# Another written order of the opening words in a fused delta-rule and hard-swish kernel

## The chip, the cores and the metric

The kernel runs on one core of a Trainium2 chip. The metric is the device time of one execution in microseconds, read as the median of three runs. A core has five engines with a queue of instructions each: TensorE (PE; its weight loads are shown apart as PEld), VectorE (DVE), ScalarE (ACT), GpSimd (POOL) and SyncE (SP), which here issues nearly all transfers between HBM and SBUF. Each queue runs strictly in the order in which the instructions were written, and an instruction whose input is not there yet holds up everything behind it in its queue.

## What is computed

Two stages. The first is a delta rule: for each of 4 batches and 8 heads a 48 x 48 state is carried through 768 tokens.

```python
k_n = k / (np.linalg.norm(k, axis=-1, keepdims=True) + 1e-06)
for t in range(S):
    y[:, :, t] = np.einsum('bhd,bhde->bhe', q[:, :, t], state)
    v_old = np.einsum('bhde,bhd->bhe', state, kt)
    state = state + bt[:, :, :, None] * np.einsum('bhd,bhe->bhde', kt, vt - v_old)
```

The second takes the result as 3072 tokens of 384 numbers through a feed-forward block of width 2048 with a hard swish between its two products.

```python
h = x @ w_in                      # 384 -> 2048
relu6 = np.clip(h + 3.0, 0.0, 6.0)
g = h * relu6 / 6.0
return (g @ w_out).astype(np.float32)   # 2048 -> 384
```

q, k, v and beta come as float32; the two weight matrices come as float64.

## The kernel before

**Tiles.** The 768 tokens are cut into 24 tiles of 32 tokens; one tile of all four batches fills the 128 partitions. Within a tile the recurrence becomes products of small matrices: the scores of the keys (`sc`, L533), a strictly lower triangular matrix per head (`L`, L544), its inverse (`X`), the state's contribution (`ks`, L792), the new values (`pz`, L813), the output (`py`, L813) and the state update (`su`, L924). Tiles form groups: tile 0 alone, then tiles 1 to 4, 5 to 8 and so on. The inverse of a group is made on VectorE, 128 problems side by side, by a substitution of pairs of ops (L716/L721 for the first full group, which works on 16 x 16 halves; L745/L750 for later groups) between two large transposes (L455, L459). The halves of tiles 1 to 4 are then joined by two groups of small matmuls per tile (`join`, L670). Tile 0 has an inverse of its own, by products on TensorE (`product`, L582).

**Feed-forward.** Two tiles make a block of 256 tokens. `up` multiplies by `w_in` in 16 units per block (L980; the first block in two halves of 16 units each, words `ua` and `ub`), with one ScalarE op (L987) and one VectorE op (L990) behind each unit. `down` multiplies by `w_out` (L1140, later L1204). The PSUM tiles of `up`, `down` and of most small products share a ring of four slots, so a unit can't start before the L990 of an earlier one has read its slot.

**Weights.** Each matrix comes in 8 pieces of 768 KB (`load_w`, L323), 16 in all, as float64 words. They become float32 by bit operations: ScalarE scales the high word (L348), makes a rounding carry from it (L351) and from the low word (L353); VectorE shifts and masks the high word (L368); GpSimd adds the carry (L375). The words `a` (three to a piece) and `c` (two to a piece: L368, then L375) step through these two generators.

**What sets the order.** The opening, up to about 175 us, is written out as a string of words, `ORDER` (L23 to L41). Each word advances a named generator by one step, and so decides where the step's instructions stand in every queue at once; a count behind a star repeats it. Behind the string follow loops for tiles 5 to 23, which are planned by costs in the code. The words: `k`, `q`, `v`, `B`, `w` issue one load each (keys, queries, values, beta, a weight piece); `n` are the norms of the keys (L393 to L417), `p` the preparation of a tile (L496, L510, L518, L533, L544), `m` the mask product (L472), `b` the scaled keys (L484), `x` the inverse of tile 0 or the join of a tile, `h` the chain of a tile, `y` its output, `i1` and `i2` the substitutions of the groups 1 and 2, `ua`, `ub`, `u` the units of the feed-forward, `ra`, `rb`, `ru` the ScalarE op behind a unit, `ga`, `gb`, `gu` the VectorE op behind it, `e` an eviction, `z` and `s` settings.

The word's meaning in code:

```python
def do(word):
    if word in gens:
        next(gens[word])
    elif word[0] == "r":
        relus[word[1]].pop(0)()
    elif word[0] == "g":
        pending[word[1]].pop(0)()
...
with tc.manual_schedule():
    for word in ORDER.split():
        word, _, n = word.partition("*")
        for _ in range(int(n or 1)):
            do(word)
```

The waits between engines are put in by the framework from what each instruction reads and writes. Loads take turns on eight completion semaphores, in the order of the words.

Of the kernel before, what the change touches and what calls it, by code (L numbers as in the profile page):

```python
# [20 lines left out]


ORDER = """  # L23
k*2 B*3 k*2 n0 k*2 z B s*2 n0*6 k*2 q*2 n1 q n1 q w k p0 z*3 k n1*2 k*2 n1*2 z p0*2 s k p0*3 a k a
m0 a n2 m1 p0 x0*2 w q x0 n1 x0*3 c n2 k s p1*2 a s*2 k q s*2 x0 n2 k*2 c x0 n2 x0 w q a*3 q p1 n2
k*2 a x0 m2 p1 c p1 n2*3 b1 q b0 s p1 x0 q w x0 n2 q*2 c*2 x0 n4 k p1 k p2*2 x0*2 a c a*2 q*3 a w v
p3*2 q x0 q n4 p2*2 c p2 v n4*2 a*3 z v n4 c m3 v c p2 n4*2 q p2 k b2 h0 c h0 w a*2 h0 p4*2 a m4 p3
q*4 h0 q k w p4*2 c*2 v*2 p3 k p3*3 k*2 p4*2 v*2 p4 m6 k a w a c w i1*3 k i1*7 a i1*4 v i1*2 k b3 k
y0 c y0*3 ua*2 ra*2 i1*3 w v ga v a*3 i1*2 ua i1 h1 i1 q w ua ra ua i1 ra*2 ga i1 k ua a ra ga i1 ga
ua ra ua ra i1 ga i1*4 ua ga n5 x1*2 k x1 c a ra v a ga x2 k*2 ga*2 ua*2 x1 ra*2 x1*2 ua h1*2 n5 k  # L30
ga ra ga*2 h1 c y1*2 ua ra w ga ua ra x2 n5 ga y1*2 ua ra ga h1 v*3 n5*2 k y1*2 ua ra x2 ub*2 n5
rb*2 h1 x3 ga c a*2 w a h2 y2 v gb ub rb gb x2 gb ub*2 n5*2 b4 rb n5 x2*2 h2 gb rb gb m5 n5*2 ub rb
gb v c q*2 v q*5 n5 ub n5 rb gb h2 y2 c h2 q ub y2*2 rb ub p5 b5 h2 rb gb*2 a*2 x3 p5 ub y2*2 k p5*2
h2 rb h3 p5 gb h3 ub*2 q rb gb rb gb ub a x3 p6 v x4 x3 rb gb ub p7 rb gb y3 c*2 v p7*2 y3 v p7*2 b6
x3 q x3 ub h3 p6*2 c p5*2 rb gb k m7 w p6 h3 u p6 k*2 q*3 a*2 y3 a p6 c y3 v y3*2 u n9 v k q a c u*2
ru gu w k a c a*2 x4 c ru p7 a c gu k u a p7 p6 m8 u*3 a k u*2 k h3 w ru*2 a*2 gu*2 x4 c x4 k c p8 k
a*2 u ru k h3 u*2 h4 ru a b8 gu k gu y4 p8*3 u h4 k*2 c q k*9 q u p8*2 k ru k*2 gu k c n9 q u q*2 p8
k*2 b7 n9*2 x4 i2 u x4 q i2*2 q ub ru gu u rb gb i2*2 h4*2 u*2 i2 ru i2*6 y4 i2 gu i2*7 u i2 ru gu
i2 u*3 ru i2*4 gu ru i2*2 v i2 gu u*4 ru c i2 u*2 i2 gu i2*3 q i2*5 y4 n9 i2 e*2 n9*2 i2*4 q i2 y4 e
n9 u ru i2*3 u h4 i2 ru*2 gu h4 u n9 i2*2 u i2 e i2*6 y4 u k n9*3 u gu i2 y4 n9 i2 p9 q i2*2 gu  # L40
"""  # L41


# [1478 lines left out]
```

## Time and profile before

| | |
|---|---|
| median of three runs | 671.5 us (671.26 to 672.24) |
| the profiled execution | 669.61 us |
| its span, first to last instruction | 667.8 us |
| PE busy | 635.8 us (95%) |
| DVE busy | 462.8 us (69%) |
| ACT busy | 260.5 us (39%) |
| POOL busy | 227.5 us (34%) |
| mean granted TensorE clock | 0.986 |

By stretches, busy time of each engine, the clock granted to TensorE and the share of the DMA engines:

| us | PE | DVE | ACT | POOL | clock | DMA |
|---|---|---|---|---|---|---|
| 0 to 10 | 1.80 | 5.01 | 3.73 | 6.56 | 1.00 | 0.57 |
| 10 to 20 | 6.10 | 5.78 | 7.39 | 5.72 | 1.00 | 1.08 |
| 20 to 30 | 7.32 | 5.70 | 7.99 | 7.16 | 1.00 | 0.86 |
| 30 to 40 | 4.24 | 5.72 | 5.81 | 7.49 | 0.73 | 0.97 |
| 40 to 50 | 7.29 | 6.04 | 7.00 | 4.90 | 0.76 | 0.78 |
| 50 to 60 | 7.65 | 9.21 | 5.59 | 0.94 | 0.75 | 0.99 |
| 60 to 70 | 9.97 | 7.48 | 6.47 | 3.96 | 0.90 | 0.51 |
| 70 to 80 | 9.35 | 5.54 | 6.92 | 1.84 | 1.00 | 0.16 |
| 110 to 120 | 10.00 | 4.81 | 6.95 | 6.97 | 1.00 | 0.43 |

How to read it: a wait is shown with what ended it. "issue" names a wait for nothing that the profile shows. A row of the order of time has the start, the duration, the engine, the line of the program, the operation, the tiles it writes and reads, and in brackets the idle time just before it with its releaser. A float32 matmul of the program is recorded as two matmuls and two weight loads.

### The profile page before, as it was taken

How to read it: one execution, taken by the hardware profiler on the slowest of the kernel's cores; microseconds unless marked ns; L12 is line 12 of the kernel's file. 1: busy time of each engine (PE TensorE's matmuls, PEld its weight loads, DVE VectorE, ACT ScalarE, POOL GpSimd, SP SyncE). 2: the span in 40 equal slices, each digit the busy share in tenths (PEclk: the TensorE clock that was granted, in tenths of full speed). 3: DMA queues.
4: the chain of work that ended last, by engine and by line, in shares of the span. 5: the costliest groups of instructions: out<-in, count | busy, mean ns of one | idle time of the engine just before them, and what ended most of it. 6: DMA issues, size and time to landing. Idle time of an engine off the chain costs nothing.

```text
span 667.8 us, 26310 instructions
## 1 busy us (share of the span) xinstructions
PE 635.8 (95%) x11544; PEld 568.2 (85%) x11544; DVE 462.8 (69%) x1110; ACT 260.5 (39%) x516; POOL 227.5 (34%) x336
## 2 busy tenths in 40 slices
PE   2768999999999999999999999999999999999997
PEld 2657887776689988988999989999999999999997
DVE  5658653689545687747888857988748998456353
ACT  4765677322142232232244244245244144153250
POOL 5762144202511130363165255055052241331330
PEclk9967999999999999999999999999999999999999
DMA  7887355302040030031030030020020020000000
GB/s 175 201 213 208 77 112 137 69 13 46 17 91 14 3 73 3 2 76 34 3 70 7 2 67 9 2 62 2 3 49 2 2 50 2 19 21 3 26 1 25
DMA packets 88499, 33.27 MB, mean 50 GB/s; under 512 B 80160, under 2 KB 83232, under 8 KB 88384
## 3 DMA queue, kind: packets, MB, share of 16 engines
q1 hardware_dynamic: 88128, 31.29, 20.9%
q8 instruction: 91, 1.49, 0.9%
q10 hardware_dynamic: 256, 0.30, 0.2%
q14 instruction: 24, 0.20, 0.1%
HBM read 26.84 MB, written 4.72 MB: 47 GB/s over the span
## 4 chain that ended last, share of the span: by engine, by line
PE 92%; DVE 2%; SPq 2%; DMA 2%; issue 1%; ACT 1%; DVEq 0%; ACTq 0%
PE po L1204 28%; PE ph L1052 21%; PE ph L980 16%; PE po L1140 6%; PE ks L792 3%; PE pt L510 3%; PE pz L813 3%; PE su L924 3%; PE py L813 3%; PE sc L533 3%; PE yt L859 1%; SPq L168 1%; DMA spare<-in_moe_w_in_dram 1%; PE pi L670 1%; DMA w_out<-in_moe_w_in_dram 1%
## 5 line engine op out<-in xcount | busy, mean ns | idle before, releaser
L1052 PE MATMUL ph<-xT,w_in 128*128 128x128 f32 (+1 forms) x560 | 121.3, 321 | 0.7 <-issue 0.7
L980 PE MATMUL ph<-xT,w_in 128*128 128x256 f32 (+1 forms) x576 | 118.7, 357 | 3.2 <-DVE g L990 2.2
L1204 PE MATMUL po<-w_out,g 128*128 128x192 f32 x640 | 110.6, 326 | 0.0
L980 PEld LDWEIGHTS ph<-xT,w_in 128*128 128x128 f32 x576 | 96.9, 197 | 15.9 <-DVE g L990 2.6
L1204 PEld LDWEIGHTS po<-w_out,g 128*128 128x128 f32 x640 | 104.6, 190 | 0.5
L1052 PEld LDWEIGHTS ph<-xT,w_in 128*128 128x128 f32 x560 | 91.1, 191 | 6.0 <-issue 0.8
L1016 POOL TENSOR_TENSOR g<-g 128x256 f32<-128x256 f32 x112 | 67.9, 608 | 82.9 <-ACT g L1066 78.5
L1204 PE MATMUL po<-spare,g 128*128 128x192 f32 x480 | 86.7, 332 | 0.0
L1204 PEld LDWEIGHTS po<-spare,g 128*128 128x128 f32 x480 | 77.2, 190 | 1.8
L987 ACT ACTIVATE g<-ph,halves 128x256 f32<-128x256 f32 (+1 forms) x96 | 41.8, 437 | 84.6 <-PE ph L980 84.5
L1214 POOL TENSOR_TENSOR o<-o,u 128x192 f32<-128x192 f32 x18 | 13.2, 732 | 175.7 <-ACT o L1211 97.2
L1066 ACT ACTIVATE g<-ph 128x512 f32<-128x512 f32 x56 | 33.5, 597 | 82.2 <-PE ph L1052 82.2
L990 DVE SCALAR_TENSOR_TENSOR g<-g,ph 128x256 f32<-128x256 f32 (+1 forms) x96 | 35.1, 371 | 40.3 <-ACT g L987 40.1
L1190 DVE TENSOR_TENSOR g<-g 128x512 f32<-128x512 f32 x80 | 55.6, 716 | 5.6 <-PE po L1204 5.6
L745 DVE TENSOR_TENSOR pr<-A 128x30 f32<-128x30 f32 (+9 forms) x150 | 57.4, 383 | 2.7
L750 DVE TENSOR_TENSOR A<-A,pr 128x30 f32<-128x30 f32 (+9 forms) x150 | 56.2, 375 | 3.7
L1079 DVE TENSOR_TENSOR g<-ph,g 128x256 f32<-128x256 f32 x56 | 23.5, 420 | 39.0 <-PE ph L1052 32.2
L1211 ACT ACTIVATE o<-po 128x192 f32<-128x192 f32 x40 | 13.2, 331 | 83.2 <-PE po L1204 79.6
L1140 PE MATMUL po<-w_out,g 128*128 128x384 f32 x128 | 45.2, 491 | 0.0
L1093 DVE SCALAR_TENSOR_TENSOR g<-o,g 128x512 f32<-128x512 f32 x56 | 40.7, 726 | 5.9 <-ACT o L1090 5.9
L1090 ACT ACTIVATE o<-g,halves 128x512 f32<-128x512 f32 x56 | 40.4, 722 | 7.6 <-DVE g L1093 5.7
L1052 PE MATMUL ph<-beta_tok,sums_in 128*128 128x128 f32 x224 | 43.3, 275 | 0.0
(144 smaller groups left out, 980.5 us busy)
## 6 DMA issues: line engine op xcount, KB each, us to landing
kf<-in_k_dram SPq DMA_DIRECT2D x96, 48.0 KB, 2.7
qb<-in_q_dram SPq DMA_DIRECT2D x96, 48.0 KB, 2.4
vf<-in_v_dram SPq DMA_DIRECT2D x96, 48.0 KB, 2.0
out_dram<-o SPq DMA_DIRECT2D x92, 48.0 KB, 1.6
spare<-in_moe_w_in_dram SPq DMA_DIRECT2D x4, 768.0 KB, 6.1
w_out<-in_moe_w_in_dram SPq DMA_DIRECT2D x4, 768.0 KB, 6.4
w_out<-in_moe_w_out_dram SPq DMA_DIRECT2D x4, 768.0 KB, 6.9
spare<-in_moe_w_out_dram SPq DMA_DIRECT2D x4, 768.0 KB, 5.7
```

Source lines behind the costliest of these rows:

```text
L745: nc.vector.tensor_tensor(out=pv, in0=A[:, j + 1 :, j].unsqueeze(2).to_broadcast([n, w, j]), in1=A[:, j, 0:j].unsqueeze(1).to_broadcast([n ...
L750: nc.vector.tensor_tensor(out=A[:, j + 1 :, 0:j], in0=A[:, j + 1 :, 0:j], in1=pv, op=ALU.subtract)
L813: nc.tensor.matmul(ps[rows(place(b)), D * h : D * h + D], lhsT=m(h)[rows(b)], rhs=z[rows(b), D * at(h) : D * at(h) + D], start=True, stop= ...
L980: nc.tensor.matmul(ph[:, cols], lhsT=w_in[:, s, f * 128 : (f + 1) * 128], rhs=xT[:, s, cols], start=(s == 0), stop=(s == NKT - 1),)
L987: nc.scalar.activation(out=g, in_=ph, func=ACTF.Relu, bias=half, scale=1.0 / 6.0)
L1016: nc.gpsimd.tensor_tensor(out=out, in0=a, in1=b, op=op)
L1052: nc.tensor.matmul(ph[:, n], lhsT=w, rhs=x, start=start, stop=stop, skip_group_check=True)
L1090: nc.scalar.activation(out=r, in_=g, func=ACTF.Relu, bias=half, scale=1.0 / 6.0)
L1093: nc.vector.scalar_tensor_tensor(out=g, in0=r, scalar=1.0, in1=g, op0=ALU.min, op1=ALU.mult)
L1140: nc.tensor.matmul(pos[c][:], lhsT=gs[blk, f // 2][:, f % 2, c * P : (c + 1) * P], rhs=w_out[:, f, :], start=(f == 0), stop=(f == NFC - 1),)
L1190: nc.vector.tensor_tensor(out=A(f, *out, 4), in0=A(f, *a, 4), in1=A(f, *b, 4), op=op)
L1204: nc.tensor.matmul(ps[n][:], lhsT=A(f - f % 2, *a)[:, f % 2], rhs=b[:, f], start=(f == 0), stop=(f == HF - 1),)
```

## The change

Only the string `ORDER` is replaced. The new string has the same 750 words, each as often as before, in another sequence; it has two lines of text more, so every later line of the program has a number higher by two (L368 becomes L370). Nothing else is edited.

```diff
--- before.py
+++ after.py
@@ -21,23 +21,25 @@
 
 
 ORDER = """
-k*2 B*3 k*2 n0 k*2 z B s*2 n0*6 k*2 q*2 n1 q n1 q w k p0 z*3 k n1*2 k*2 n1*2 z p0*2 s k p0*3 a k a
-m0 a n2 m1 p0 x0*2 w q x0 n1 x0*3 c n2 k s p1*2 a s*2 k q s*2 x0 n2 k*2 c x0 n2 x0 w q a*3 q p1 n2
-k*2 a x0 m2 p1 c p1 n2*3 b1 q b0 s p1 x0 q w x0 n2 q*2 c*2 x0 n4 k p1 k p2*2 x0*2 a c a*2 q*3 a w v
-p3*2 q x0 q n4 p2*2 c p2 v n4*2 a*3 z v n4 c m3 v c p2 n4*2 q p2 k b2 h0 c h0 w a*2 h0 p4*2 a m4 p3
-q*4 h0 q k w p4*2 c*2 v*2 p3 k p3*3 k*2 p4*2 v*2 p4 m6 k a w a c w i1*3 k i1*7 a i1*4 v i1*2 k b3 k
-y0 c y0*3 ua*2 ra*2 i1*3 w v ga v a*3 i1*2 ua i1 h1 i1 q w ua ra ua i1 ra*2 ga i1 k ua a ra ga i1 ga
-ua ra ua ra i1 ga i1*4 ua ga n5 x1*2 k x1 c a ra v a ga x2 k*2 ga*2 ua*2 x1 ra*2 x1*2 ua h1*2 n5 k
-ga ra ga*2 h1 c y1*2 ua ra w ga ua ra x2 n5 ga y1*2 ua ra ga h1 v*3 n5*2 k y1*2 ua ra x2 ub*2 n5
-rb*2 h1 x3 ga c a*2 w a h2 y2 v gb ub rb gb x2 gb ub*2 n5*2 b4 rb n5 x2*2 h2 gb rb gb m5 n5*2 ub rb
-gb v c q*2 v q*5 n5 ub n5 rb gb h2 y2 c h2 q ub y2*2 rb ub p5 b5 h2 rb gb*2 a*2 x3 p5 ub y2*2 k p5*2
-h2 rb h3 p5 gb h3 ub*2 q rb gb rb gb ub a x3 p6 v x4 x3 rb gb ub p7 rb gb y3 c*2 v p7*2 y3 v p7*2 b6
-x3 q x3 ub h3 p6*2 c p5*2 rb gb k m7 w p6 h3 u p6 k*2 q*3 a*2 y3 a p6 c y3 v y3*2 u n9 v k q a c u*2
-ru gu w k a c a*2 x4 c ru p7 a c gu k u a p7 p6 m8 u*3 a k u*2 k h3 w ru*2 a*2 gu*2 x4 c x4 k c p8 k
-a*2 u ru k h3 u*2 h4 ru a b8 gu k gu y4 p8*3 u h4 k*2 c q k*9 q u p8*2 k ru k*2 gu k c n9 q u q*2 p8
-k*2 b7 n9*2 x4 i2 u x4 q i2*2 q ub ru gu u rb gb i2*2 h4*2 u*2 i2 ru i2*6 y4 i2 gu i2*7 u i2 ru gu
-i2 u*3 ru i2*4 gu ru i2*2 v i2 gu u*4 ru c i2 u*2 i2 gu i2*3 q i2*5 y4 n9 i2 e*2 n9*2 i2*4 q i2 y4 e
-n9 u ru i2*3 u h4 i2 ru*2 gu h4 u n9 i2*2 u i2 e i2*6 y4 u k n9*3 u gu i2 y4 n9 i2 p9 q i2*2 gu
+k*3 s z B q s k B q B q k B q n0 w n0 k n0 k*3 s n0*4 k*2 z p0 k m1 p0*4 n1*2 z w m0 q k n1 z p0 a k
+a p0 x0 n1 x0 n1 a q k x0 k n2 x0*2 k n2 s c w n1 b0 a c n2 s a q*2 n2 n1 x0 k a*2 x0*3 n2 q x0 n2 q
+p1 n2*2 k p1 x0 k n4 x0 b1 p1 w n4 z q n2 v n4*2 x0 q p2 q*3 a w c v p2*2 x0 q v a c p3 p1 k c p1 b2
+n4 b3 a x0 k x0 p1 c a n4 v p2 p1 a c w p2 k s p3 n4 p2 q h0 a q m2 h0 p4 p2 p3 a c h0 q p4 q w p3 c
+v a*2 q m3 p4*2 p3 h0 a v p4 k w c a z p3 a v p4 y0 v c y0 p3 m4 q p4 i1*2 y0 k y0 s c ua i1*3 k a
+i1*2 c i1 k a i1*2 k i1 w ua c ra i1 k i1 ra ua i1*2 ra v ga h1 i1 v w a*2 i1 ua ra i1*2 a v ga i1
+ua*2 ra i1 ga k ra i1 w i1 v c i1*2 ua c ga k i1*2 a ga ra i1 ua i1 ra i1 ga i1 x1 y1 ua x1 ga ua x1
+a ra m5 ga n5 ga x2 a h1 x1 ra q ua ga ra ua n5 x1 n5 ua k x1 ga c n5 c n5 x2 h1*2 y1 v n5 ua y1 ra
+q k ra ga k ga k v ua x3 a y1*2 a k y1 h1 ra n5 ub rb w ga gb ra x2 ub rb h1 a x2 q*2 ga ua v*2 ub
+n5 ra rb ga c gb ub b4 n5 h2 ub s x2 rb n5 rb gb n5 h2 y2 gb ub x2 h2 a q h2 n5*2 v k gb m6 ub rb q
+y2 p5 b5 ub x4 gb rb p6 h2 k rb c ub q ub v a gb y2 gb a p5 q x3 rb gb rb y2 gb q k h2 q p5 ub c k
+x3 x4 x3 ub rb w p7 y2 a gb p7 rb b6 p6 h3 k gb y2 a p6 p5 v ub a v h3 w p8 p5 k p7 rb ub x3 gb ub
+rb c y3 rb x3 s gb p5 p7 gb y3 c h3 q n9 u q h3 v p5 q k n9 a p7 k p6 y3 p7 k y3 a y3 c p6 u y3 q*2
+v m7 u p6 u ru k p7 gu a k b8 x4*2 k p6 n9 a u*2 a k ru h3 q n9 u gu u ru gu k ru u q u k m8 k gu u
+h3 ru p8 gu h4*2 k u p8*2 a y4 u ru p8*2 y4 n9 c n9 c w p8 a gu u x4 c i2*3 k u a k x4 u ru*2 u k i2
+c gu k w n9 u h4 gu n9 a i2*2 h4 ub u i2 c rb q ru i2*3 gb i2 n9 c i2 u i2 u ru i2 a i2*2 q i2 k
+i2*2 h4 i2 gu i2 c gu i2*2 a i2 u*2 q ru i2 u i2 h4 i2*2 gu ru k n9 u i2 a q u*2 gu ru u k i2 q ru
+i2 gu i2 c i2 q k*2 i2 u i2 n9 y4 u i2*4 e b7 u i2 k y4 e i2 y4 gu ru k n9 v u e i2*3 n9 k i2 k*2 p9
+q v i2*2 u i2 e u i2 gu q u i2*6 k i2 ru i2*4 q y4 i2 gu u i2
 """
```

## The prediction

> **What bounds the kernel now.** First the page: the busy tenths of the 40 slices, the clock row, and the DMA kinds.
>
> ```profile
> PE   2768999999999999999999999999999999999997
> PEclk9967999999999999999999999999999999999999
> q8 instruction: 91, 1.49, 0.9%
> ```
>
> From the fifth slice (67 us) TensorE is full. All its idle time but about 6 us lies before that, so an order of the opening words can only move the opening. Of 32 us of idle time (667.8 less 635.8) some 28 lie before 105 us. The third line is the fetching of the engines' own instructions: 91 packets of 16 KB that share the DMA engines with the loads.
>
> Then TensorE's instructions in order of time, with the wait before each in brackets.
>
> ```profile
> 34.04 0.27 PE L533 MATMUL sc<-KQ 64*32 64x64 f32 x2 [1.80 <-issue]
> 40.26 0.45 PE L924 MATMUL su<-R,sums_in 32*64 32x48 f32 x3 [2.94 <-issue]
> 52.41 0.79 PE L792 MATMUL ks<-state,KQ 64*64 64x48 f32 x37 [0.56 <-issue]
> 55.85 6.61 PE L980 MATMUL ph<-xT,w_in 128*128 128x128 f32 x30 [1.79 <-DVE g L990]
> 62.39 0.73 PE L670 MATMUL pi<-X,sums_in 16*32 16x16 f32 x64
> ```
>
> Three waits are on nothing but the instruction stream; they lie 127 and 255 recorded matmuls apart, in the middle of a group. The last row is the point where the opening ends: the first matmuls of a joined inverse (I call it the join). From there to the end TensorE waits only 1.8 us in the opening and some 4 at the close. So the forecast is: when does the join come, and how much work is left behind it.
>
> Then the same stretch on VectorE and GpSimd.
>
> ```profile
> 47.53 1.96 DVE L455 STREAM_TRANSPOSE A<-L 128x1024 f32<-128x1024 f32 x1
> 49.52 1.17 DVE L716 TENSOR_TENSOR pr<-A 128x28 f32<-128x28 f32 x1
> 50.73 0.21 DVE L721 TENSOR_TENSOR A<-A,pr 128x28 f32<-128x28 f32 x1
> ...
> 60.69 0.44 DVE L680 STREAM_TRANSPOSE sums_in<-X 128x256 f32<-128x256 f32 x1
> ```
>
> ```profile
> 31.62 1.81 POOL L375 TENSOR_TENSOR w_in<-w_in,spare 128x768 int32<-128x768 int32 x1 [2.41 <-ACT root L403]
> ...
> 48.84 1.81 POOL L375 TENSOR_TENSOR w_in<-w_in,spare 128x768 int32<-128x768 int32 x1
> ```
>
> Rows of VectorE that read two operands from SBUF (L408, L412, L716, L721) stretch when a GpSimd add is running: L716 takes 1.17 us where its neighbours take 0.21, and ends as the add of 48.84 ends; the L408 of 32.23 takes 1.23 us against 0.17 and ends with the add of 31.62. L455 (1.96, as without an add) and the ops with a PSUM operand (L544, L590, L990) do not stretch. Before this change the whole substitution chain (L716/L721, 28 ops between the two 32x32 transposes) meets one add, and only its tail: 0.96 us.
>
> **The change part by part.** Both orders hold the same 750 words with the same counts, so every instruction stays; only positions move, up to some 175 us, and the loops behind them are alike. TensorE's work is therefore constant and the sum is a sum of waits up to the join. I write A for the start of L455, T for the end of L680; before, A = 47.53, T = 61.13 and the join 62.39 (1.26 late, since at the half clock of 56 to 62 us each unit of six matmuls takes 1.3 us).
>
> Loads. Eight completion lanes are handed out in turn, beta's four included, and an issue waits for the load eight earlier (the load queue's issue of 16.30 follows the landing, at 16.28, of the piece of 10.14). Before, a weight piece is the sixth to eighth load after the last one, so pieces overlap; now pieces 0 to 3 sit exactly eight apart and each waits for the one before. Piece 0 goes at about 5.2 instead of 6.65 (q's last load now ahead of k's second tile), then by the old durations (12.25-6.65 = 5.6, 16.28-10.14 = 6.1) they land near 10.8, 17, 23, 28, and 4 to 6 near 32, 37.5, 42.5. Before, ScalarE stood waiting for them at 12.25, 16.31, 21.72, 32.42 and 38.26. So piece 2 costs ScalarE 1.3 us more, piece 5 about 0.8 less. The first k tile is issued one slot later (0.49) and the second tile's square root moves behind the first tile's two copies on ScalarE, with the reduce that needs it ahead of the first mask product on VectorE: that product starts near 13.2 instead of 12.14. By the end of the first inverse (L642, 29.73 before) this is made good, since its copy no longer stands behind the conversion of piece 2: about 29.5. The third sc group now stands behind one more conversion (0.9+1.07+1.05): its first 62 matmuls end near 34.6, where before they ended at 32.24 and waited for instructions until 34.04.
>
> The end of su. pz and the copy take 34.8 to 36.6, su 1.27 more: 37.8 if instructions are there. The next block was fetched from 34.04 to 40.26 before, 6.2 us with two pieces under way; now it is asked for near 34.8, with piece 5 under way and piece 6 issued near 34.5. Bounds 37.8 and 42.6 (behind piece 6); I take 40.5, the nearest row being that 6.2: -0.2.
>
> From su to A. Before, 6.83 us: transposes, four copies, two sc groups, four products and piece 6's L368 (0.94). Now 5.65: transposes 1.1 (as at 40.64), copies 0.6 and 0.6, one L351 that is moved between them (1.0), a copy 0.6, the last sc 0.85, two products 0.8. Gain 1.15; A = 46.15.
>
> From A to T. The conversions of pieces 6 and 7 (L368, 0.92 each; one before A, one after T until now) stand between ops of the chain: +1.84. Each releases its GpSimd add (1.81) right there, the next chain op reads two SBUF operands, and nothing else of VectorE stands in front of it: +3.62. GpSimd's two mask products (L472, 0.59 each) follow the second add and take about one more op's wait: +0.6. The tail of 0.96 that was there goes: -0.96. So T = A + 13.6 + 5.1 = 64.85. The bounds of the add's cost: nothing, if it finds the chain in a transpose, up to the whole 1.81; the two rows above, both blocked to the add's end, put me at the whole.
>
> In the Trainium skill, "SBUF — State Buffer", section "Who interferes with whom", a VectorE instruction with two SBUF inputs and a GpSimd instruction that reads SBUF exclude each other for a whole instruction. By that rule both adds cost the full 1.81, as taken; by the one chain row of 0.96 apiece the sum would be 1.7 us less.
>
> The join. TensorE, with four PSUM slots, has done its units by then and starts at T: -1.26. One more unit of six matmuls stands ahead of the join (L980: ten units instead of nine) and is done in the wait: -0.67 (half of 2.27 less 0.94). Behind the join, R's three ops and three L990 now precede the corner product, so the second join group starts about 3.05 after the first instead of 2.30, with the same two units between: +0.6. The clock is low again while TensorE waits for L990, and it is full only after some 6 us without gaps (55.85 to 62): +0.5, between 0 and 2.
>
> Sum: -0.2 -1.15 +1.84 +3.26 -1.26 -0.67 +0.6 +0.5 = +2.9 us. Against the profiled execution (669.6, span 667.8 plus 1.8) that is 672.5; the median shown lies 1.9 above it, so **674.4**.
>
> Later conversions cost nothing by this count. Pieces 12 to 15 were done before the next chain (L455 at 127.95); now 14 and 15 stand within it: two L368 and two adds, at most +3.4. Their cover: pz waits for that chain's X; it started at 165.24 with the chain's R ready at 163.78 (1.5 slack), and between the sc group that opens the chain and this pz there are now one unit more (1.3) and two po matmul pairs more (1.3), and A stands 0.5 closer. 4.6 us of cover; without it 3.4 would come on top. The mask, norm and scaled words that move from GpSimd's early queue, and the k and q loads behind them on SP, land in the stretches from 100 us where TensorE has no wait on them.
>
> **The rivals.**
>
> Level: the instruction blocks come in time. Then su ends at 37.8, but ScalarE's conversion of piece 4 and its wait for piece 5 stand before the copy that feeds the last sc; A comes no earlier than 44.4. 1.75 and the cold half microsecond come off: 670.3, median 672.2. For it: piece 6 is issued at about the time of the request, not before. Against: all four waits of 1.80, 2.94, 0.56 and 0.94 fall in stretches with pieces under way, as here. In the Trainium skill, "Runtime: NRT & Kernel Launch", section "Instruction fetch mechanics", crossing an instruction block is said to be mostly hidden; by that this case would be the likeliest, and the three rows shown speak against it.
>
> Faster: the loads run quicker one at a time. If a piece alone takes the 4.6 us of piece 3 (19.48 to 24.1), pieces 2 to 5 land 3 to 5 us sooner, ScalarE never stands waiting and the instruction blocks pass between pieces. It decides once piece 5 lands before 34: A is then bounded by ScalarE's own conversions, about 41.5. 4.65 and 0.5 off: 667.3, median 669.2. For it: 54 to 63 GB/s in 26 to 28 and 32 to 34 us show room. Against: the rest of 8 to 40 us runs at 200 to 300 GB/s.
>
> Much slower: the block waits behind piece 6, su ends at 42.6 and the chain follows: +2.1, median 676.5; with the cover of the second chain gone as well, up to 680.
>
> **How the numbers follow.** Forecast 0.40, much slower 0.18, level 0.17, faster 0.25. Hence slower by over 0.2% (1.3 us, about what three runs between 671.3 and 672.2 can tell) 0.58, within 0.17, faster 0.25. The range takes in the faster case and most of the slower one: 668.5 to 679.5; the forecast's own is 670.2 (both adds and the mask products at nothing, 4.2 off) to 676.5 (su's end at its upper bound).
>
> **What would show it.** Weight pieces 0 to 3 issued each at the landing of the one before; the sc and su waits on issue still there, su ending at 40 to 41; A near 46; inside the chain two single ops of 1.5 us or more, each ending with a GpSimd add; the join near 65 (62.39 before) and TensorE full behind it; no wait of pz near 168. The prediction is wrong if those two ops last 0.3 us, if A comes before 44, or if TensorE waits over 2 us between the join and 180 us.

## The result and the profile after

The changed kernel takes 675.96 us (median of four executions, 675.1 to 677.54) against 671.38 for the kernel before on the same chip: ratio 1.0074, 95% interval 1.0046 to 1.0102. It is 4.6 us slower. The forecast was 674.4, slower. The profiled execution of the changed kernel is the slowest of its four (677.54, span 675.8), 7.9 us above the profiled one of before; its single rows are read with that in mind.

The page first: the busy tenths, the clock row and the DMA kind of instructions.

```profile
PE   2778899999999999999999999999999999999997
...
PEclk9957899999999999999999999999999999999999
...
q8 instruction: 91, 1.49, 1.0%
```

TensorE is full one slice later than before (from the sixth on, 84 us, instead of the fifth). Now the changed kernel's TensorE in order of time; in brackets the wait ahead of a group and what ended it.

```profile
34.23 0.30 PE L535 MATMUL sc<-KQ 64*32 64x64 f32 x2 [0.54 <-issue]
...
38.70 0.45 PE L926 MATMUL su<-R,sums_in 32*64 32x48 f32 x4 [0.50 <-issue]
...
45.54 0.63 PE L535 MATMUL sc<-KQ 64*32 64x64 f32 x18 [1.45 <-issue]
...
65.17 0.86 PE L672 MATMUL pi<-X,sums_in 16*32 16x16 f32 x64
...
67.77 0.72 PE L672 MATMUL pi<-X,sums_in 32*32 32x16 f32 x64 [0.19 <-DVE sums_in L690]
...
78.43 3.75 PE L982 MATMUL ph<-xT,w_in 128*128 128x128 f32 x19 [2.28 <-issue]
82.12 1.35 PE L794 MATMUL ks<-state,KQ 64*64 64x48 f32 x64
...
98.47 0.55 PE L794 MATMUL ks<-state,KQ 64*64 64x48 f32 x20 [1.45 <-issue]
```

The join (first group of L672) comes at 65.17 instead of 62.39. Behind it there are two long waits on nothing but instructions, 2.28 and 1.45, where the kernel before had one of 0.94:

```profile
99.75 0.80 PE L813 MATMUL py<-R,LB 32*32 32x48 f32 x56 [0.94 <-issue]
```

They matter twice. TensorE stands still meanwhile; and after the wait of 2.28 the next 19 matmuls of L982 take 3.75 us (2.39 in other profiles of this order), because the clock of that stretch is low, 0.69. The windows around it, with TensorE's busy time first and clock, DMA share and GB/s last:

```profile
70.00:76.00 6.00, 6.00 (x234) 5.34 (x222) 3.09 (x10) 4.57 (x11) 3.10 (x6) 1.00 0.68 182
76.00:78.43 2.43, 0.15 (x2) 0.00 (x0) 1.67 (x5) 0.00 (x0) 0.00 (x0) 1.00 0.37 69
78.43:84.00 5.57, 5.57 (x88) 5.29 (x89) 2.12 (x8) 2.48 (x6) 0.00 (x0) 0.69 0.01 3
```

VectorE and GpSimd, in the substitution chain:

```profile
46.95 1.94 DVE L457 STREAM_TRANSPOSE A<-L 128x1024 f32<-128x1024 f32 x1
...
50.31 0.94 DVE L370 TENSOR_SCALAR w_in<-spare 128x768 uint32<-128x768 uint32 x1
...
51.73 1.78 DVE L718 TENSOR_TENSOR pr<-A 128x100 f32<-128x100 f32 x1
53.55 0.27 DVE L723 TENSOR_TENSOR A<-A,pr 128x100 f32<-128x100 f32 x1
...
57.58 0.94 DVE L370 TENSOR_SCALAR w_in<-spare 128x768 uint32<-128x768 uint32 x1
...
58.70 1.86 DVE L723 TENSOR_TENSOR A<-A,pr 128x72 f32<-128x72 f32 x1
...
60.68 0.57 DVE L718 TENSOR_TENSOR pr<-A 128x52 f32<-128x52 f32 x1
61.29 0.54 DVE L723 TENSOR_TENSOR A<-A,pr 128x52 f32<-128x52 f32 x1
...
64.49 0.45 DVE L682 STREAM_TRANSPOSE sums_in<-X 128x256 f32<-128x256 f32 x1
```

```profile
51.59 1.80 POOL L377 TENSOR_TENSOR w_in<-w_in,spare 128x768 int32<-128x768 int32 x1 [5.65 <-ACT spare L355]
58.67 1.80 POOL L377 TENSOR_TENSOR w_in<-w_in,spare 128x768 int32<-128x768 int32 x1 [5.27 <-DVE pr L718]
...
60.57 1.19 POOL L474 TENSOR_TENSOR mb<-beta_tok,mask 128x256 f32<-128x256 f32 x2
```

Each of the two conversions (L370, 0.94) is followed by its GpSimd add (L377, 1.80), 0.34 and 0.15 us after its end (the first add is released, by the profile, by ScalarE's last step for that piece). The chain operation that starts next lasts until that add has ended: 1.78 instead of 0.27, 1.86 instead of 0.23. The mask products of 60.57 stretch two more (0.57 and 0.54 for 0.21). T is 64.94.

The weight loads on SP's queue:

```profile
5.18 0.45 SPq L325 DMA_DIRECT2D spare<-in_moe_w_in_dram  x1
...
10.38 0.39 SPq L325 DMA_DIRECT2D spare<-in_moe_w_in_dram  x1
...
15.85 0.38 SPq L325 DMA_DIRECT2D w_out<-in_moe_w_in_dram  x1
...
21.12 0.39 SPq L325 DMA_DIRECT2D w_out<-in_moe_w_in_dram  x1
...
71.95 0.41 SPq L325 DMA_DIRECT2D spare<-in_moe_w_out_dram  x1
```

The first four wait for one another, as forecast. The last one shown, piece 11, goes out 4 us before TensorE runs dry at 76.15.

### The profile page after: what moved, and what is told of

It is laid out like the page before. It is cut to its first block, busy times and chain, and to the rows that moved or that the text cites. A ratio compares the mean times of both kernels' runs of the same rounds, so it can differ in the third digit from the quotient of the medians.

```text
span 675.8 us, 26309 instructions
## 1 busy us (share of the span) xinstructions
PE 642.2 (95%) x11544; PEld 572.7 (85%) x11544; DVE 468.4 (69%) x1110; ACT 260.0 (38%) x516; POOL 227.8 (34%) x336
## 4 chain that ended last, share of the span: by engine, by line
PE 89%; DMA 7%; DVE 1%; issue 1%; ACT 1%; SPq 0%; ACTq 0%; DVEq 0%
PE po L1206 28%; PE ph L1054 21%; PE ph L982 15%; PE po L1142 6%; PE ks L794 4%; PE pz L815 3%; PE py L815 3%; DMA spare<-in_moe_w_in_dram 3%; PE su L926 3%; PE pt L512 3%; PE sc L535 2%; DMA w_out<-in_moe_w_in_dram 2%; DMA vf<-in_v_dram 2%; PE yt L861 1%; DMA w_out<-in_moe_w_out_dram 1%
## 5 line engine op out<-in xcount | busy, mean ns | idle before, releaser
L982 PE MATMUL ph<-xT,w_in 128*128 128x256 f32 (+1 forms) x576 | 121.1, 362 | 5.8 <-issue 2.5
L982 PEld LDWEIGHTS ph<-xT,w_in 128*128 128x128 f32 x576 | 98.0, 200 | 18.9 <-issue 3.5
L747 DVE TENSOR_TENSOR pr<-A 128x30 f32<-128x30 f32 (+9 forms) x150 | 60.2, 401 | 2.8
L752 DVE TENSOR_TENSOR A<-A,pr 128x30 f32<-128x30 f32 (+9 forms) x150 | 58.4, 389 | 3.6
L520 ACT ACTIVATE KQ<-pt 128x512 f32<-128x512 f32 x48 | 28.4, 594 | 40.7 <-PE pt L512 40.3
```

Source lines behind the costliest of these rows:

```text
L747: nc.vector.tensor_tensor(out=pv, in0=A[:, j + 1 :, j].unsqueeze(2).to_broadcast([n, w, j]), in1=A[:, j, 0:j].unsqueeze(1).to_broadcast([n ...
L752: nc.vector.tensor_tensor(out=A[:, j + 1 :, 0:j], in0=A[:, j + 1 :, 0:j], in1=pv, op=ALU.subtract)
L982: nc.tensor.matmul(ph[:, cols], lhsT=w_in[:, s, f * 128 : (f + 1) * 128], rhs=xT[:, s, cols], start=(s == 0), stop=(s == NKT - 1),)
```

## The experiments

All ratios are against executions of the kernel before on the same chip, taken alongside; each has an interval of about plus or minus 0.25%, 1.7 us. A single execution of either kernel strays by 2.1 us (standard deviation; 35 executions of the kernel before lie between 667.9 and 676.3), so rows of one profile are evidence for mechanisms, and times come from the ratios.

My theory after reading the trace had two causes: the chain (conversions and blocked operations, forecast) and the instruction blocks behind the join, which wait behind bursts of loads (not forecast). Excerpts of the written order show each edit; a word `c` is a conversion step (VectorE's L370, then GpSimd's add L377), `w` a weight load, `a` a ScalarE step of a conversion, `i1` a step of the chain, `x1` one of the join.

**out_both: the conversions of pieces 6 and 7 out of the chain.**

```diff
-i1*2 c i1 k a i1*2 k i1 w ua c ra i1 k i1
+i1*3 k a i1*2 k i1 w ua ra i1 k i1
...
-i1 v c i1*2 ua c ga k i1*2 a ga
+i1 v i1*2 ua ga k i1*2 ga
...
-x1 a ra m5 ga n5 ga x2 a h1 x1 ra q ua ga ra ua n5 x1 n5 ua k x1
+x1 ra m5 ga n5 ga x2 h1 x1 c ra q c a*3 ua ga ra ua c n5 x1 n5 ua k c x1
```

> The changed kernel with the four conversion words of pieces 6 and 7 (two on VectorE, two adds on GpSimd) taken out of the substitution chain and put behind the second half of the join; the first part of piece 8's conversion on ScalarE moves behind them. Theory (the chain's two conversions and two blocked operations set the loss): T, the end of the transpose L682, comes from 64.9 to 59.2-60, the first join group from 65.2 to 61.5-62.5, and the time from 676.0 to 672.3-673.3. Rival (the loads and the instruction fetches after the join set the loss, the chain is covered): T moves but the time stays above 675.

Measured: 675.53, ratio 1.0066 (1.0039 to 1.0093). No gain that can be told. The chain did shrink: T minus A is 13.40 instead of 17.99. But TensorE's rows behind the join of this kernel show what was late next:

```profile
47.75 0.51 PE L535 MATMUL sc<-KQ 64*32 64x64 f32 x18 [2.81 <-issue]
...
62.66 0.73 PE L672 MATMUL pi<-X,sums_in 16*32 16x16 f32 x64 [1.24 <-DVE g L992]
...
65.27 0.72 PE L672 MATMUL pi<-X,sums_in 32*32 32x16 f32 x64 [0.33 <-DVE sums_in L690]
67.97 1.27 PE L982 MATMUL ph<-xT,w_in 128*128 128x128 f32 x6 [1.98 <-POOL w_in L377]
70.77 1.50 PE L815 MATMUL pz<-R,X 32*32 32x48 f32 x64 [1.54 <-ACT X L698]
```

The unit at 67.97 needs piece 6, which is now converted only after the join: 1.98 us of waiting for GpSimd's add, and 1.54 for the join's own next copy. And this execution had lost 2.81 at an instruction block before the chain began, so A was 49.04. The edit exchanged one stall for another. What the rival foretold is what came (T moves, the time stays above 675), but with the new stalls in it the run doesn't decide between the two.

**out_last: only the last add behind the chain.**

```diff
-i1*2 ua c ga k
+i1*2 ua ga k
...
-ga n5 ga x2 a h1
+ga n5 ga c x2 a h1
```

> The changed kernel with only the last GpSimd add (piece 7) moved behind the chain; its VectorE conversion stays. Theory: one blocked operation of 1.86 us becomes 0.25, T and the join come 1.3 to 1.6 earlier, the time is 674.4 to 674.8. If the adds do not block (the long operations had another reason), an operation of over 1.5 us stays in that place and the time stays at 676.

Measured: 676.64, ratio 1.0080 (1.0054 to 1.0106). The edit did nothing, and GpSimd's row beside VectorE's says why:

```profile
57.93 1.80 POOL L377 TENSOR_TENSOR w_in<-w_in,spare 128x768 int32<-128x768 int32 x1 [4.98 <-DVE pr L718]
```

```profile
57.96 1.86 DVE L723 TENSOR_TENSOR A<-A,pr 128x72 f32<-128x72 f32 x1
```

Between the old and the new place of the add GpSimd has only the two mask products (and memsets), and those now run earlier; the add still starts when its conversion ends, and the chain's next operation is blocked for 1.86 as before. Where the add takes place is set by where VectorE's conversion stands. So an operation of over 1.5 us stays in its place, but not because adds do not block: the add itself has not moved. (In the changed kernel two chain operations lie between the first conversion and the long one, and they take their usual 0.24 and 0.25; it is the add that the long one goes with.) The run counts as a second sample of the changed kernel.

**load_later: weight piece 11 eight loads later.**

```diff
-n5 ub rb w ga gb
+n5 ub rb ga gb
...
-n5*2 v k gb m6 ub
+n5*2 v k w gb m6 ub
```

> The changed kernel with one load word moved: weight piece 11, issued at 71.95 in a burst of eight loads, goes eight loads later on SP's queue (about 84 to 86). Every compute engine has the same instructions in the same order. Theory (the wait of 2.28 at 78.43 is an instruction block queued behind that burst, and the half clock of 79 to 83 follows from it): the wait falls below 0.5, the clock stays full, the time falls by 3 to 4 to 672-673. Rival (the wait belongs to the stream, not to the loads): the wait stays at 2 or more and the time within 0.5 of 676.

Measured: 674.41, ratio 1.0044 (1.0017 to 1.0071), against 1.0074 and 1.0080 for the changed kernel and out_last; the intervals overlap. The 672 to 673 expected did not come, and a gain is not shown. Piece 11 goes out at 82.31 instead of 71.95, and the block that cost 2.28 costs 0.39. But the next ones grow:

```profile
77.19 2.39 PE L982 MATMUL ph<-xT,w_in 128*128 128x128 f32 x19 [0.39 <-issue]
...
95.03 0.55 PE L794 MATMUL ks<-state,KQ 64*64 64x48 f32 x20 [0.91 <-issue]
...
100.34 0.68 PE L535 MATMUL sc<-KQ 64*32 64x64 f32 x43 [0.96 <-issue]
```

Counted from 58 to 185 us, the waits on issue sum to 3.37 (3.93 in the changed kernel's profile). The clock stays full from 70 us on, which is worth 1.6 us against the changed kernel's profile (L982's 19 matmuls take 2.39 instead of 3.75, the ks group behind them 1.15 instead of 1.35). The wait does follow the burst; but the burst has to go somewhere.

**in_both: the same four words put into the chain of the kernel before.**

```diff
-a c w i1*3 k i1*7 a i1*4 v i1*2 k b3 k y0 c y0*3
+a w i1*3 k i1*4 c i1*3 a i1 c i1*3 v i1*2 k b3 k y0*4
...
-q w ua ra ua i1 ra*2 ga i1 k ua a
+c q w ua ra ua i1 ra*2 ga i1 c k ua a
...
-x1 c a ra v
+x1 a ra v
...
-h1 c y1*2 ua
+h1 y1*2 ua
```

> The kernel before with the same four words put into its chain, at the places that they have in the changed kernel; nothing else moves. Theory: two operations of the chain of 1.5 us or more, A about 0.9 earlier, T 3.6 to 4.3 later (61.1 to 65), the join 2.3 to 3.1 later, the time from 671.4 to 673.5-674.7. Rival (the chain is covered by TensorE's other work): less than 0.7 more.

Measured: 672.62, ratio 1.0028 (1.0000 to 1.0056): 1.9 us more than before, with an interval that reaches down to nothing, and less than the 673.5 to 674.7 expected. VectorE's chain and the join in that kernel:

```profile
46.21 1.94 DVE L455 STREAM_TRANSPOSE A<-L 128x1024 f32<-128x1024 f32 x1
...
49.58 0.95 DVE L368 TENSOR_SCALAR w_in<-spare 128x768 uint32<-128x768 uint32 x1
...
50.72 1.88 DVE L721 TENSOR_TENSOR A<-A,pr 128x88 f32<-128x88 f32 x1
...
57.32 0.95 DVE L368 TENSOR_SCALAR w_in<-spare 128x768 uint32<-128x768 uint32 x1
...
58.52 1.80 DVE L721 TENSOR_TENSOR A<-A,pr 128x72 f32<-128x72 f32 x1
```

```profile
64.71 0.88 PE L670 MATMUL pi<-X,sums_in 16*32 16x16 f32 x64
```

T minus A is 17.77 (13.60 before), the join 2.3 later. A is 1.3 us earlier, which takes back part of it. By its best estimate the chain is worth some 2 us in this order, not all of the 4.6; by itself this run does not show a loss clear of the noise.

**again: the changed kernel once more, as the yardstick of the three that follow.**

> The changed kernel itself once more, as the yardstick of the three others of this call: 1.005 to 1.010 of the kernel before.

Measured: 674.70, ratio 1.0064 (1.0039 to 1.0090).

**out_tail: the conversion of piece 6 at the end of the chain, that of piece 7 behind the join.**

```diff
-i1*2 c i1 k a i1*2 k i1 w ua c ra i1 k i1
+i1*3 k a i1*2 k i1 w ua ra i1 k i1
...
-i1 v c i1*2 ua c ga k i1*2 a ga ra i1 ua i1 ra i1 ga i1 x1 y1
+i1 v i1*2 ua ga k i1*2 ga ra i1 ua i1 c ra i1 ga i1 x1 c a y1
...
-h1 x1 ra q ua ga ra ua n5 x1 n5 ua k x1
+h1 x1 c ra q ua ga ra ua n5 x1 n5 ua k c x1
```

> The changed kernel with piece 6's conversion at the very end of the chain, so that its GpSimd add lies under the transpose L461, and piece 7's behind the second half of the join; this mends the fault of the first attempt, where TensorE waited for piece 6 right behind the join. Theory (the two conversions and the two blocked operations in the chain are a real part of the loss): no operation of the chain over 0.6 us, T minus A from 18.0 to 13.2-14.3, the first join group 2 to 3.5 earlier against its A, and the time 2 to 3 us under that of the unchanged kernel of this call. Rival (covered by TensorE's units at the half clock): the join moves by under 1 and the time by under 1.

Measured: 671.48, ratio 1.0017 (0.9992 to 1.0042), 0.47% or 3.2 us under `again`. VectorE's and TensorE's rows:

```profile
45.23 1.95 DVE L457 STREAM_TRANSPOSE A<-L 128x1024 f32<-128x1024 f32 x1
...
55.25 0.94 DVE L370 TENSOR_SCALAR w_in<-spare 128x768 uint32<-128x768 uint32 x1
...
56.32 1.96 DVE L461 STREAM_TRANSPOSE X<-A 128x1024 f32<-128x1024 f32 x1
58.32 0.45 DVE L682 STREAM_TRANSPOSE sums_in<-X 128x256 f32<-128x256 f32 x1
```

```profile
58.99 0.73 PE L672 MATMUL pi<-X,sums_in 16*32 16x16 f32 x64 [1.60 <-DVE g L992]
```

The conversion still stands in the chain (0.94 at 55.25), but its add lies under the transpose of 56.32, which takes 1.96 as ever. T minus A is 13.54, the join comes at 58.99. This is what the first attempt should have been.

**load_apart: pieces 11 and 13 both later.** The edit of load_later, and:

```diff
-v h3 w p8 p5 k
+v h3 p8 p5 k
...
-q k n9 a p7
+q k w n9 a p7
```

> The changed kernel with two load words moved: weight piece 11 as in the run before, and piece 13, which followed piece 12 by 2.8 us, eight loads later. Compute engines unchanged. Theory (instruction blocks queue behind bursts of loads): the waits on issue near 77 and 97 each below 0.6, no half clock after 70, the time 2.5 to 4 us under the unchanged kernel. Rival (the waits only move on to the next block): the sum of the waits on issue between the join and 110 stays at 3 to 4 us and the gain is under 1.

Measured: 674.70, ratio 1.0051 (1.0029 to 1.0072). The gain of 0.13% can't be told from none. The wait near 97 is gone, and a new one stands where piece 13 (now issued at 98.62) is under way:

```profile
105.19 0.80 PE L815 MATMUL py<-R,LB 32*32 32x48 f32 x57 [1.86 <-issue]
```

From 58 to 185 the waits on issue sum to 2.61 (2.79 in `again`). That is less than the 3 to 4 that the rival named, but in its main point the rival was right: they move on to another block, and the time stays.

**tail_apart: both edits.**

> Both of these edits together. If the chain and the bursts are the two causes and add up, 4 to 6.5 us under the unchanged kernel, so within about 1 us of the kernel before on either side. If one of them covers the other, 2.5 to 3.5 under.

Measured: 670.80, ratio 0.9990 (0.9963 to 1.0018): no different from the kernel before, and some 5 us under `again`. out_tail alone had 0.47% of these 0.74%; the 0.27% between out_tail and both edits lies within the noise, and the profiled execution, one of 676.14, still has 3.95 of waits on issue from 58 to 185. What is shown of the gain is the chain's.

**thin_before and thin_after: the late weight pieces without their bytes.**

```diff
+        few = slice(0, 8 if i >= 6 else P)
         nc.sync.dma_start(
-            out=raws[i].rearrange("p s f z -> p s (f z)"), in_=src.bitcast(U32)
+            out=raws[i].rearrange("p s f z -> p s (f z)")[few], in_=src.bitcast(U32)[few]
         )
```

Pieces 6 to 15 load 8 of their 128 partitions, so 15/16 of their bytes are left out and the output is not the reference's; pieces 0 to 5 come whole.

> The kernel before, with weight pieces 6 to 15 cut to 8 of their 128 partitions: the loads keep their places, lanes and waits, but 15/16 of their bytes are left out, so the weights of those pieces are not the reference's (they hold what lay there), and the instructions that convert them stay. Theory (blocks of instructions queue behind the bytes of the loads): of the waits on issue, that of su (2.94) falls under 1 and those near 52 and 99 under 0.2; the time falls from 671 to 666-669, and its spread from run to run (2.1 us) shrinks. Rival (the waits belong to the stream): they stay, the time within 1 of 671.

> The changed kernel with the same pieces cut in the same way. Theory: the waits at 45, 78 and 98 fall under 0.3 each and the half clock after 78 goes; what is left of the difference between the two orders is the chain, 2 to 3.5 us more than the thin kernel before: 669-671.5. Rival (the waits belong to the order): the sum of the waits on issue behind the join stays above 2.5 and the difference at 4 to 5.

Measured: thin_before 669.06, ratio 0.9947 (0.9923 to 0.9972); thin_after 670.30, ratio 0.9982 (0.9959 to 1.0004). Behind the join the waits on issue are all but gone: none from 58 to 185 in thin_before, one of 0.36 in thin_after. So there they are made by the bytes of the weight pieces. With the bytes gone the two orders lie 2.4 us apart (their intervals just overlap) instead of 4.3 (`again`) to 4.6.

The wait of su did not follow the theory. Its rows in the two kernels (thin_before first; L925 and L927 are the su line):

```profile
40.09 0.44 PE L925 MATMUL su<-R,sums_in 32*64 32x48 f32 x3 [3.31 <-issue]
```

```profile
38.94 0.45 PE L927 MATMUL su<-R,sums_in 32*64 32x48 f32 x4 [2.69 <-issue]
```

The wait did not shrink: 3.31 where three kernels with the old opening and all bytes had 2.94 (before), 3.36 (before_tail) and 3.51 (in_both), and 2.69 where those with the new opening had 0.50 to 2.10. The bytes of piece 6 can't be what that block waits for in these kernels. Two things are still under way at that time: the loads of k, q and v, of 48 KB each (in thin_before 1900 of the 1957 packets from 36.8 to 40.1 us are under 512 bytes, and the DMA engines are nine tenths busy until 38.6), and the end of piece 5, which kept all its bytes and for which ScalarE waits until 38.58 in thin_before. Whether either makes the wait was not tried. The spread from run to run did not shrink in thin_before either (2.0 us; 1.4 in thin_after).

**thin_tail: out_tail without the bytes.**

> The changed kernel with piece 6's conversion at the end of the chain and piece 7's behind the join, and the same pieces cut. If chain and bursts are all that parts the two orders, it equals the thin kernel before within 1 us; if a third cause is left it is over 1.5 us slower.

Measured: 666.53 (six executions), ratio 0.9913 (0.9883 to 0.9942). That is 2.3 us faster than thin_before, not within 1, and not slower as the other reading had it. The two intervals overlap a little (0.9923 to 0.9942), but five of the six executions lie under eleven of the twelve of thin_before: a third term is likely there, and it is a gain. In the two profiles A is 44.98 against 47.67 and the join 58.71 against 61.99, which puts the gain into the opening; no run isolates it.

**before_tail: the kernel before with piece 6's conversion at the end of its chain.**

```diff
-a c w i1*3 k
+a w i1*3 k
...
-b3 k y0 c y0*3
+b3 k y0*4
...
-i1 k ua a ra ga i1
+i1 k ua ra ga i1
...
-i1*4 ua ga n5
+i1*2 c i1*2 c a ua ga n5
```

> The kernel before with piece 6's conversion moved from before the chain to its end, as in the best variant of the changed kernel; all bytes are loaded. A comes 0.9 earlier, the blocked operation of 1.17 us is gone, T comes about 1 earlier. Since TensorE reached the join 1.3 after T before, most of it is covered: the time 0 to 0.8 us under the kernel before.

Measured: 671.13, ratio 0.9985 (0.9961 to 1.0010). In its profile T is 59.82 and the join 59.87 instead of 62.39, yet 2.60 us of waits on issue (1.10 before) follow it. No gain that can be told.

**The sum.** Each step starts at the kernel where another ends, so that they add up to the whole: the changed order without chain and bytes against the old one without bytes, -0.34% (2.3 us gained); its chain put back, from thin_tail to thin_after, +0.69% (4.6 us; these two intervals do not overlap); the bytes put back, +0.82% in the changed order and +0.53% in the old one, 1.9 us of difference. -2.3 + 4.6 + 1.9 = +4.2, the +0.64% of `again`. That it closes is arithmetic; the single terms carry an error of some 2 us, and only the chain is well outside it (out_tail shows it a second time, at 3.2).

## Why the prediction was right, and where it was not

**Loads.** Right: pieces 0 to 3 go out at 5.18, 10.38, 15.85 and 21.12, each at the landing of the one before. Pieces 0 to 2 take 5.2 to 5.5 us apiece and piece 3 takes 6.8, not the 4.6 that the rival of quicker single loads needed, and A never came near its 41.5.

**The end of su.** Forecast 40.5, bounds 37.8 and 42.6. In the eight profiles of kernels with this opening and all bytes it lies between 38.11 and 40.12, mean 38.9: the wait is there in all of them, but 0.5 to 2.1 long, and not the 2.7 that 40.5 held (40.5 less 37.8). The old order has 40.1 to 40.7. The reason given, that the block lies behind piece 6, fell with the thin kernels. So "much slower" had no ground, and "level", which needed blocks that come in time, met its condition in none of the eight.

**From su to A.** Forecast 5.65, measured 7.5 on the mean of the eight (5.40 to 9.14). The step left out the next block, in the middle of the last sc group (45.54 above): 0 to 3.03, mean 1.5. What is left of the difference, 0.4, has no cause shown. The two errors, 1.6 early and 1.85 late, cancel by luck: A is 46.4 on the mean (43.65 to 49.04), forecast 46.15; once, in `again`, it came before the 44 that the text named as a sign against itself.

**From A to T.** Forecast 18.7; 17.99 in the changed kernel, 18.01 to 18.18 in four more profiles with this chain. Both adds blocked to their end, both conversions 0.94, the masks 0.69. Too high by 0.5 to 0.7, mostly because the own time of each of the two blocked operations, 0.23 and 0.27, was counted on top of the add's 1.81. In the Trainium skill, "SBUF — State Buffer", section "Who interferes with whom", a VectorE instruction with two SBUF inputs and a GpSimd instruction that reads SBUF exclude each other. Every add that starts inside a chain here agrees (operations of 1.78 to 1.90), and the transposes, with one input, kept their 1.96 under an add in out_tail.

**The join.** Right: 0.23 behind T (1.26 before), near 65 (62.05 to 65.17 in the five profiles with this chain). The second group follows 2.60 later, not 3.05, in the profile shown and in out_last, but 3.83 or 3.84 in `again`, load_later and load_apart. There the clock was still half behind the first group (0.50 from 62 to 66 in `again`). So the allowance for the clock, 0.5 with bounds of 0 and 2, is a term that changes by 1.2 from execution to execution.

**"TensorE full behind it".** This is the step that failed. Later words were costed at nothing, and the text named over 2 us of waiting between the join and 180 as its own refutation. It came: 3.93 us in the profiled execution, 2.79 and 2.21 in two others (`again` and out_last), against 1.10 and 1.02 in the old order (2.60 in before_tail). What makes these waits is shown: the bytes of the w_out pieces, without which 0 to 0.36 is left. Before, pieces 8 to 11 are issued by 59 us, while TensorE waits for the chain anyway, and 12 to 15 at 67.17, 93.40, 100.84 and 107.15; after, piece 11 too goes out behind the join, at 71.95, and pieces 12 and 13 within 2.8 us, at 91.52 and 94.28, into a full TensorE whose next instruction block comes over the same DMA engines. Once, it also cost the half clock, 1.6 us. How much of the median they make is less sure: no run that moved the loads gained anything by it that is clear of the noise.

**Pieces 14 and 15 in the second chain.** Right: pz starts at 172.59 without a wait.

**The sum.** In the terms of the experiments the forecast had -1.35 for the opening, +4.3 for the chain and what follows it at the join, and nothing for the blocks behind it. The runs give -2.3, +3.2 to +4.6, and +1.9. The sign was right, and so was the mechanism of the chain, the largest term. The opening came 1 us better and the omitted term 1.9 worse; with errors of some 2 us on each, it is in part luck that the median lies only 1.6 us above the forecast.

## What to carry to other kernels

A conversion that hands work to GpSimd should stand where VectorE's next operation is a transpose or has a PSUM operand: the same work cost 3.2 us less with one conversion at the end of the chain and the other behind the join than with both inside it, while moving the GpSimd instruction alone changed nothing. When loads are moved into a stretch where the bound engine is full, count the block crossings of its instruction stream there as a cost (here up to 2.3 us for one that met a large burst). Shifting a burst moved the wait to a later crossing here; to place it where that engine waits anyway, as the old order does with four of the pieces, is the better bet. After moving a step out of a chain, look at who needs it first behind the chain, or the stall comes back there.

## What the runs showed beyond that

The waits at instruction blocks vary from execution to execution. The same program, profiled twice (the changed kernel and `again`), had 0.50 and 1.37 us at su, 1.45 and 0 at sc; over the eight kernels with this opening that of su goes from 0.5 to 2.1 and that of sc from 0 to 3.03, and A differs by up to 5.4 us. This accompanies a spread of 2.1 us in the times; that it makes most of it is argued, not shown. In the Trainium skill, "Runtime: NRT & Kernel Launch", section "Instruction fetch mechanics", crossing a block is said to be mostly hidden. With 15/16 of the late weight bytes gone the trace agrees behind the join (0 and 0.36 us in 127 us); with them it does not (1.02 to 3.95).

The wait of 2.28 us was followed by some 3.5 us at half clock, the same block's waits of 0.94 in `again` and 1.21 in out_last by none: the next 19 matmuls took 2.39 us there. So the long wait cost 1.7 times its length (2.28 and 1.6 on top); how long a wait has to be for that was not measured.
